# Sparse attention into a routed mixture of experts: the summary scores of a head pair in one block of four array tiles

## The chip, the core and the metric

The kernel runs on one core of a Trainium2 chip. The metric is the device time of one execution in microseconds. Before the change the median of three runs is 690.34 us (690.23 to 690.6). One execution was also recorded by the hardware profiler: it took 690.0 us, of which 688.3 us lie between the first and the last instruction (the span). The rest of this document speaks of the engines by their names in the profile: PE (the matrix engine, with PEld for its weight loads), DVE (vector), ACT (scalar), POOL and SP.

## The reference

Two things are computed one after the other.

```python
# attention: q, k, v are (4, 8, 768, 64); block = 32, window = 16
k_sum = k.reshape(B, H, nb, 32, D).max(axis=3)      # 24 block maxima of the keys
v_sum = v.reshape(B, H, nb, 32, D).mean(axis=3)     # 24 block means of the values
scores_l = scale * q @ k.T, masked to |row - col| < 16
scores_s = scale * q @ k_sum.T + log(32)            # 24 summary scores for each query
a = softmax(concat(scores_l, scores_s)); attn = a @ concat(v, v_sum)
# routing: x = attn as (3072, 512); 8 experts, hidden size 1024
P = exp(x @ w_gate - max); 8 times: divide rows by their sums, then columns, times N / E
out = sum over e of P[:, e] * (relu(x @ w1[e]) @ w2[e])
```

The change touches `scores_s` alone: for each head a product of 24 summary keys (padded to 32 rows) with 768 queries over a head size of 64.

## The kernel before

**Attention by pairs.** There are 32 heads, taken two at a time: 16 pairs `i`, four for each batch entry. The two heads of a pair are `j = 0, 1`; the transposed keys `kT`, queries `qT` and block maxima `ksT` of head `j` lie on partitions `64*j` to `64*j+63`. The 768 queries are worked on in two halves `h` of `HS` = 384. The first four pairs (`i < PB`, `pair_half`) are done half by half; the twelve others (`pair_whole`, line 634) as a whole.

For a whole pair PE does: two transposes of keys and queries into PSUM (`tr`, L282), the window scores for each half (`scores`, L301), the block sums of the values (`block_sums`, L309), the summary scores for each half (`summaries`, L387), the values for each half (`values`, L373 and L379), and a transpose of the result (`to_xT`, L473). ACT and DVE empty PSUM between these steps: ACT computes the exponentials (`score_exp` L344, `summary_exp` L397), DVE masks, makes block maxima and normalizes, and either of them does the copies (L195).

**Summary scores.** `summaries(i, h, tag)` opens one PSUM bank and issues two matmuls, one for each head. Each uses 64 rows of the array (the head's partitions) and 32 columns (the summary keys); head 0 writes PSUM partitions 0 to 31, head 1 partitions 32 to 63. So the two matmuls lie in two different tiles of the array, shape 64 x 32. The other half does the same again in another bank, in the same two tiles. `summary_exp(i, h)` then takes the exponential of partitions 0 to 63 of that bank.

**PSUM banks in the attention.** Three single banks with the tag `"a"` are handed out in turn to `tr`, `block_sums`, `summaries`, `values`, `to_xT` and `logits` of the whole pairs; one double bank `"s"` belongs to the window scores; three banks `"m"` belong to expert 0.

**Expert 0 as filler.** The first expert is computed unsplit in the same stretch of time (`expert0`, line 665): eight hidden products of four matmuls each (`hd`, L199) and three projections of eight matmuls (`pj`, L204) for each 384 tokens, as soon as the tokens' attention is done. It fills PE while attention waits for the other engines.

**What sets the order.** The class `Plan` (line 34) holds a unit for each step with its engine, an assumed cost, its dependencies, a priority and the banks that it opens or uses. It plays the units through on paper and emits them in that order; each engine then executes its own units strictly in that order. A unit that opens banks is emitted only when the previous users of those banks, in turn, are planned to be done. For copies with two possible engines the plan chooses. In the plan a call of `summaries` costs 0.22 us on PE and a `summary_exp` 0.46 us on ACT.

**The bridge.** When the last attention unit has been emitted (`logits` of the fourth batch entry, L487, and the exponential of the logits, L491), `bridge` (line 997) adds the eight row and column normalizations of `P` to the plan. Each is a chain DVE (L1007, L1008), POOL (L1011), DVE (L1015), PE (`totals`, two matmul instructions at L1020), DVE (L1023), POOL (L1028). It also adds sums of the second expert's weights and of the tokens on DVE (L765, L768: `w1_sum`, `x_sum`) and that expert's first products on PE (L818: `p1`, `p5`, `p2`, `p6`, `p3`, `p7`, `p4`). The leftover units of expert 0 stand between them. After that, from 178.6 us on, a loop with a fixed order works through experts 1 to 7 (L818, L824) by a scheme with seven instead of eight products.

Of the kernel before, what the change touches and what calls it, by code (L numbers as in the profile page):

```python
# [12 lines left out]
AF = mybir.ActivationFunctionType  # L13
# [20 lines left out]
class Plan:  # L34
# [12 lines left out]
    def add(self, eng, cost, fn, deps=(), prio=0.0, opens=(), uses=(), lag=0.0):  # L47
        u = Unit(eng, cost, fn, [d for d in deps if d is not None], prio, list(opens), lag)
        for b in list(opens) + list(uses):
            b.users.append(u)  # L50
        if uses and eng != "PE":
            u.prio -= 100.0
        self.waiting.append(u)
        return u
# [62 lines left out]
def kernel(  # L117
# [10 lines left out]
    nc = tc.nc  # L128
# [10 lines left out]
    PB = H // 2  # L139
    SCALE = 1.0 / float(D) ** 0.5  # L140
    W = 16
    LIVE = 128 + 2 * W
    PADL = LIVE + 2 * W
    HS = S // 2
# [64 lines left out]
    NB = PB  # L209
    NE = 2  # L210
# [10 lines left out]
    if True:  # L221
# [4 lines left out]
        qT = [attn.tile([128, W + S + W], BF16, name=f"qT{i}") for i in range(NB)]  # L226
        kT = [attn.tile([128, S], BF16, name=f"kT{i}") for i in range(NB)]
        ksT = [attn.tile([128, 32], BF16, name=f"ksT{i}") for i in range(NB)]
# [9 lines left out]
        add = plan.add  # L238

        at, units = {}, {}  # L240

        def bank(tag, name, dtype=FP32):
            pool, n = (mps, 3) if tag == "m" else (aps, NA)
            return pool.tile([128, 2048 // mybir.dt.size(dtype)], dtype, tag=tag, name=name, bufs=n)
# [79 lines left out]
        def near_values(i):  # L324

            sv, ve = v_x[i % NQ], V_e[i % NE]
            for j in range(2):
                c0, q0 = VD * j, 64 + 32 * j
                nc.sync.dma_start(out=ve[q0 + W:q0 + 2 * W, 1:G, c0:c0 + VD],
                                  in_=sv[128 - W:128, 0:G - 1, j, :])  # L330
                nc.sync.dma_start(out=ve[q0:q0 + W, 0:G - 1, c0:c0 + VD],
                                  in_=sv[0:W, 1:G, j, :])

        def scores(i, h):
            sg = at["sg", i, h] = banks2("sg")
            for s in range(HG):
                for j in range(2):
                    score_mm(i, sg[:, j, s * LIVE:(s + 1) * LIVE], j, HG * h + s, 0, LIVE)

        def score_exp(i, h):  # L340
            if h == 0:
                at["er", i] = attn.tile([128, 2, G, LIVE], BF16, tag="er", name="er", bufs=2)
                at["em", i] = attn.tile([128, 2, G, 128], BF16, tag="em", name="em", bufs=2)
            nc.scalar.activation(  # L344
                out=at["er", i][:, :, HG * h:HG * (h + 1), :].rearrange("p j g l -> p j (g l)"),
                in_=at.pop(("sg", i, h))[:, :, 0:HG * LIVE], func=AF.Exp, bias=0.0, scale=SCALE)

        def masks(i, h):
            c = slice(HG * h, HG * (h + 1))
            nc.vector.tensor_tensor(  # L350
                out=at["em", i][:, :, c, :], in0=at["er", i][:, :, c, W:W + 128],
                in1=band[:, None, None, W:W + 128].to_broadcast([128, 2, HG, 128]), op=ALU.mult)

        def edges(i):
            ee, er = E_e[i % NE], at.pop(("er", i))
            for j in range(2):
                q0 = 64 + 32 * j
                nc.vector.tensor_tensor(out=ee[q0:q0 + 32, 0:G - 1, 128 - W:128],
                                        in0=er[0:32, j, 1:G, 0:W],
                                        in1=band[0:32, None, 0:W].to_broadcast([32, G - 1, W]),  # L360
                                        op=ALU.mult)
                nc.vector.tensor_tensor(out=ee[q0:q0 + 32, 1:G, 0:W],
                                        in0=er[96:128, j, 0:G - 1, W + 128:LIVE],
                                        in1=band[96:128, None, W + 128:LIVE].to_broadcast([32, G - 1, W]),
                                        op=ALU.mult)

        def values(i, h):
            sv, ee, ve, em = v_x[i % NQ], E_e[i % NE], V_e[i % NE], at["em", i]
            av = at["av", i, h] = bank("a", "av")
            for cc in range(HG):  # L370
                c, o = HG * h + cc, cc * 2 * VD
                for j in range(2):
                    nc.tensor.matmul(av[:, o + j * VD:o + (j + 1) * VD],  # L373
                                     lhsT=em[:, j, c, :], rhs=sv[:, c, j, :],
                                     start=(cc == 0 and j == 0), stop=False,
                                     skip_group_check=True)
            for cc in range(HG):
                c, o = HG * h + cc, cc * 2 * VD
                nc.tensor.matmul(av[:, o:o + 2 * VD], lhsT=ee[:, c, :], rhs=ve[:, c, :],  # L379
                                 start=False, stop=True, skip_group_check=True)  # L380

        def summaries(i, h, tag):
            r = i % NB
            ss = at["ss", i, h] = bank(tag, "ss")
            for j in range(2):
                p0 = 64 * j
                nc.tensor.matmul(ss[32 * j:32 * j + 32, 0:HS], lhsT=ksT[r][p0:p0 + 64, :],  # L387
                                 rhs=qT[r][p0:p0 + 64, W + h * HS:W + (h + 1) * HS],
                                 start=True, stop=True)

        def summary_exp(i, h):
            if i < PB:
                es = at["es", i, h] = attn.tile([64, HG, 128], BF16, tag="es", name="es", bufs=2)
                dst = es[:]
            else:
                dst = E_e[i % NE][0:64, HG * h:HG * (h + 1), :]
            nc.scalar.activation(out=dst.rearrange("p g t -> p (g t)"),  # L397
                                 in_=at.pop(("ss", i, h))[0:64, 0:HS], func=AF.Exp,
                                 bias=0.0, scale=SCALE)


# [165 lines left out]
        U = {}  # L567
# [66 lines left out]
        def pair_whole(i, prio):  # L634
            U["near", i] = add("SP", 0.4, lambda: near_values(i), [U["v", i], U.get(("A", i - NE, 1))], prio,
                               lag=3.5)
            for h in range(2):
                buf = Buffer("s")
                U["S", i, h] = add("PE", 0.28, lambda h=h: scores(i, h),
                                   [U["kT", i, 0], U["kT", i, 1], U.get(("ed", i - 2))], prio, opens=[buf])  # L640
                U["X", i, h] = add("ACT", 0.97, lambda h=h: score_exp(i, h), [U["S", i, h]], prio, uses=[buf])
                U["mk", i, h] = add("DVE", 0.56, lambda h=h: masks(i, h),
                                    [U["X", i, h], U.get(("A", i - 2, 1))], prio)
            U["ed", i] = add("DVE", 0.78, lambda: edges(i),
                             [U["X", i, 0], U["X", i, 1], U["mk", i, 1], U.get(("A", i - NE, 1))], prio)
            for h in range(2):
                buf = Buffer("a")
                U["ss", i, h] = add("PE", 0.22, lambda h=h: summaries(i, h, "a"),
                                    [U["km", i], U["kT", i, 1], U.get(("A", i - NE, 1))], prio, opens=[buf])
                U["sx", i, h] = add("ACT", 0.46, lambda h=h: summary_exp(i, h), [U["ss", i, h]], prio, uses=[buf])  # L650
            for h in range(2):
                buf = Buffer("a")
                U["A", i, h] = add("PE", 0.4, lambda h=h: values(i, h),
                                   [U["mk", i, h], U["ed", i], U["sx", i, h], U["Vs", i], U["near", i]],
                                   prio, opens=[buf])
                U["no", i, h] = add("DVE", 0.68, lambda h=h: normalize(i, h),
                                    [U["A", i, h], U.get(("xt", i - 2))], prio, uses=[buf])
            buf = Buffer("a")
            U["xt", i] = add("PE", 0.35, lambda: to_xT(i), [U["no", i, 0], U["no", i, 1]], prio, opens=[buf])
            U["x", i] = add({"ACT": 0.8, "DVE": 0.9}, 0, lambda: x_out(U["x", i].on, i), [U["xt", i]], prio,  # L660
                            uses=[buf])
# [88 lines left out]
    if True:  # L750
# [340 lines left out]
        for n in range(LAG, len(groups)):  # L1091
# [3 lines left out]
            e, j, i = groups[n]  # L1095
# [61 lines left out]
        A, B, C, D = last  # L1157
# [42 lines left out]
```

## Time and profile before

| what | value |
|---|---|
| median of the runs | 690.34 us |
| profiled execution | 690.0 us, span 688.3 us |
| PE busy | 675.2 us (98%) |
| DVE busy | 588.1 us (85%) |
| ACT busy | 404.8 us (59%) |
| granted PE clock | 0.999 of full speed |
| summary score matmuls (L387) | 64, from 8.7 us to 120.9 us |
| last expert-0 matmul (L204) ends | 178.6 us |

A table by windows gives the busy time of each engine in each stretch, with the number of instructions behind it. The chain of waits lists, in order of time, the pieces of work that led to the last instruction: its start, its length, engine, tile and line. A timeline lists instructions with their start and length, and in square brackets the idle time of the engine before them and what ended it. A shape such as `64*32` is the part of the array that a matmul uses, rows by columns.

### The profile page before, as it was taken

To read this page: it belongs to the slowest core of one execution; us is meant where nothing else is said; L and a number is where in the kernel's file an instruction comes from. 1 tells how busy PE (TensorE), PEld (TensorE's weight loads), DVE (VectorE), ACT (ScalarE), POOL (GpSimd) and SP (SyncE) were. 2 spreads that over 40 slices of the span, in tenths; PEclk is the share of its full clock that TensorE was granted. 3 is DMA by queue.
4 is the path that set the end of the run, shared out by engine and by line. 5 is a ranking of instruction groups with operands and counts; after the bars stand their busy time and mean duration, and the time that the engine had idled before them with its cause. 6 is when DMAs were issued, how large, how long until landed. Compare 5 with 4: busy or idle time off the path is not lost.

```text
span 688.3 us, 13623 instructions
## 1 busy us (share of the span) xinstructions
PE 675.2 (98%) x5195; PEld 438.9 (64%) x5195; DVE 588.1 (85%) x1436; ACT 404.8 (59%) x785; POOL 140.7 (20%) x189
## 2 busy tenths in 40 slices
PE   8999999899999999999999999999999999999996
PEld 4665665445566666666666666666666666666665
DVE  6878888687599998899789988998799988998886
ACT  4677866555677775555555555555555555555551
POOL 9599920121113120110101010201010101100000
PEclk9999999999999999999999999999999999999999
DMA  9999990000233104130513050403231051301224
GB/s 131 182 131 127 128 130 6 1 1 0 31 48 32 17 7 70 17 32 1 77 12 37 1 77 1 46 2 50 28 32 16 3 75 16 32 1 47 83 88 153
DMA packets 112785, 33.90 MB, mean 49 GB/s; under 512 B 98128, under 2 KB 109904, under 8 KB 112720
## 3 DMA queue, kind: packets, MB, share of 16 engines
q0 software_dynamic: 103840, 26.22, 40.0%
q1 hardware_dynamic: 8352, 6.80, 3.3%
q8 instruction: 41, 0.67, 0.4%
q14 instruction: 24, 0.20, 0.1%
q10 hardware_dynamic: 528, 0.02, 0.0%
HBM read 52.45 MB, written 6.29 MB: 85 GB/s over the span
## 4 chain that ended last, share of the span: by engine, by line
PE 87%; DVE 11%; issue 2%; ACT 0%; DVEq 0%; ACTq 0%
PE xy L824 32%; PE pg L818 14%; PE pb L818 10%; PE pa L818 9%; PE yps L204 6%; PE hps L199 6%; DVE hf L768 3%; DVE out_acc L961 2%; PE sg L301 1%; PE tkq L282 1%; PE idle L511 1%; DVE hf L879 1%; PE ss L387 1%; PE vs L309 1%; PE tx L473 1%
## 5 line engine op out<-in xcount | busy, mean ns | idle before, releaser
L824 PEld LDWEIGHTS <-hf 128*128 128x128 f16 x2352 | 229.7, 98 | 99.2 <-issue 5.2
L824 PE MATMUL xy<-w,hf 128*128 128x256 f16 x1312 | 183.3, 272 | 0.0
L824 PE MATMUL xy<-ws,hf 128*128 128x256 f16 x984 | 147.5, 272 | 1.4
L190 ACT ACTIVATE hf<-pg 128x512 f16<-128x512 f32 x84 | 50.1, 597 | 159.6 <-PE pg L818 159.6
L961 DVE SCALAR_TENSOR_TENSOR out_acc<-xy,P_sb,out_acc 128x512 f32<-128x512 f32 x164 | 114.9, 741 | 1.7 <-PE xy L824 1.7
L765 DVE TENSOR_TENSOR hf<-hf 128x512 f16<-128x512 f16 x252 | 99.3, 421 | 3.1
L818 PE MATMUL pa<-xT,w 128*128 128x512 f16 x336 | 99.9, 379 | 0.0
L768 DVE TENSOR_TENSOR hf<-pb,c 128x512 f16<-128x512 f32 x84 | 58.0, 690 | 36.8 <-ACT xy L943 31.1
L818 PEld LDWEIGHTS <-w 128*128 128x128 f16 x672 | 65.7, 98 | 28.3 <-issue 0.5
L175 POOL DMA_DIRECT2D w<-in_moe_w_dram x56 | 42.3, 821 | 187.0 <-PE pg L818 181.5
L818 PEld LDWEIGHTS <-ws 128*128 128x128 f16 x504 | 49.3, 98 | 42.2
L190 ACT ACTIVATE hf<-pa 128x512 f16<-128x512 f32 x84 | 50.1, 597 | 21.4 <-PE pa L818 21.4
L768 DVE TENSOR_TENSOR hf<-pg,c 128x512 f16<-128x512 f32 x84 | 57.1, 679 | 0.4 <-PE pg L818 0.2
L837 ACT COPY pg<-pa 128x512 f32<-128x512 f32 x84 | 47.9, 570 | 5.1 <-PE pa L818 0.3
L818 PE MATMUL pg<-xTs,w 128*128 128x512 f16 x168 | 49.9, 379 | 0.1
L845 ACT COPY c<-pb 128x512 f32<-128x512 f32 x84 | 49.7, 592 | 0.4 <-ACT pg L837 0.4
L818 PE MATMUL pb<-xTs,ws 128*128 128x512 f16 x168 | 50.0, 379 | 0.0
L818 PE MATMUL pg<-xTs,ws 128*128 128x512 f16 x168 | 50.0, 379 | 0.0
L818 PE MATMUL pb<-xT,ws 128*128 128x512 f16 x168 | 50.0, 379 | 0.0
L818 PE MATMUL pg<-xT,w 128*128 128x512 f16 x168 | 49.8, 377 | 0.0
L852 ACT COPY c<-pg 128x512 f32<-128x512 f32 x84 | 48.7, 580 | 0.0
L199 PE MATMUL hps<-xT,w 128*128 128x384 f16 x256 | 48.6, 326 | 0.0
(133 smaller groups left out, 862.1 us busy)
## 6 DMA issues: line engine op xcount, KB each, us to landing
w<-in_moe_w_dram POOLq DMA_DIRECT2D x8, 1024.0 KB, 9.3
w<-in_moe_w_dram POOLq DMA_DIRECT2D x56, 128.0 KB, 3.5
out_dram<-out_acc SPq DMA_DIRECT2D x22, 256.0 KB, 2.0
vx<-in_v_dram POOLq DMA_DIRECT2D x32, 96.0 KB, 5.4
kst<-in_k_dram POOLq DMA_DIRECT2D x24, 96.0 KB, 4.6
qst<-in_q_dram POOLq DMA_DIRECT2D x24, 96.0 KB, 4.3
w<-in_moe_w_dram POOLq DMA_DIRECT2D x2, 512.0 KB, 8.4
kst<-in_k_dram POOLq DMA_DIRECT2D x4, 192.0 KB, 4.5
```

The lines of the kernel that those rows point to most:

```text
L175: nc.gpsimd.dma_start(out=t[:, :, h, :], in_=moe_w1[e].rearrange("(dk p) f -> p dk f", p=128)[:, :, f:f + 128])
L190: nc.scalar.activation(out=out, in_=in_, func=AF.Relu, bias=0.0, scale=1.0)
L199: nc.tensor.matmul(hp[:, 0:n], lhsT=w1s[e][:, dk, 128 * f:128 * (f + 1)], rhs=xT[:, dk, t0:t0 + n], start=(dk == 0), stop=(dk == KD - 1))
L204: nc.tensor.matmul(yp[:], lhsT=h[:, f, c * 128:(c + 1) * 128], rhs=w2s[e][:, f, :], start=(f == 0), stop=(f == KF - 1))
L765: nc.vector.tensor_tensor(out=out, in0=in0, in1=in1, op=ALU.subtract)
L768: nc.vector.tensor_tensor(out=out, in0=in0, in1=in1, op=ALU.add)
L818: nc.tensor.matmul(bank[:], lhsT=w[:, dk, :], rhs=x[:, dk, :], start=start and dk == 0, stop=dk == KH - 1, skip_group_check=True)
L824: nc.tensor.matmul(bank, lhsT=a(f)[:, 128 * c:128 * (c + 1)], rhs=w[:, f, :], start=start and f == 0, stop=f == FH - 1, skip_group_check=True)
L837: nc.scalar.copy(out=B["g"][:], in_=B["a"][:])
L845: nc.scalar.copy(out=B["c5"][:], in_=B["b"][:])
L852: nc.scalar.copy(out=B["c2"][:], in_=B["g"][:])
L961: nc.vector.scalar_tensor_tensor(out=acc, in0=src, scalar=P_sb[:, t, e:e + 1], in1=acc, op0=ALU.mult, op1=ALU.add)
```

## The change

For whole pairs the two calls of `summaries` become one call of `summaries2(i)`, which opens two banks and issues all four matmuls: half 0 writes partitions 0 to 63 of the first bank, half 1 partitions 64 to 127 of the second. The four matmuls lie in four different tiles of the array. `summary_exp` reads half 1 from partitions 64 to 127. In the plan there is one PE unit of 0.22 us in the place of two, which opens both banks; the two ACT units stay, each on its bank. The first four pairs are as before. The matmuls are the same in number and size.

```diff
+        def summaries2(i):
+            r = i % NB
+            ss = at["ss", i, 0], at["ss", i, 1] = bank("a", "ss"), bank("a", "ss")
+            for h in range(2):
+                for j in range(2):
+                    p0, o = 64 * j, 64 * h + 32 * j
+                    nc.tensor.matmul(ss[h][o:o + 32, 0:HS], lhsT=ksT[r][p0:p0 + 64, :],
+                                     rhs=qT[r][p0:p0 + 64, W + h * HS:W + (h + 1) * HS],
+                                     start=True, stop=True)
         def summary_exp(i, h):
+            o = 64 * h if i >= PB else 0
...
-                                 in_=at.pop(("ss", i, h))[0:64, 0:HS], func=AF.Exp,
+                                 in_=at.pop(("ss", i, h))[o:o + 64, 0:HS], func=AF.Exp,
...
+            bufs = [Buffer("a"), Buffer("a")]
+            U["ss", i, 0] = U["ss", i, 1] = add("PE", 0.22, lambda: summaries2(i),
+                                                [U["km", i], U["kT", i, 1], U.get(("A", i - NE, 1))], prio,
+                                                opens=bufs)
             for h in range(2):
-                buf = Buffer("a")
-                U["ss", i, h] = add("PE", 0.22, lambda h=h: summaries(i, h, "a"),
-                                    [U["km", i], U["kT", i, 1], U.get(("A", i - NE, 1))], prio, opens=[buf])
-                U["sx", i, h] = add("ACT", 0.46, lambda h=h: summary_exp(i, h), [U["ss", i, h]], prio, uses=[buf])
+                U["sx", i, h] = add("ACT", 0.46, lambda h=h: summary_exp(i, h), [U["ss", i, h]], prio,
+                                    uses=[bufs[h]])
```

## The prediction

> **What bounds the kernel now.** I first read busy time by stretches of 20 us, to see where PE, which does the changed work, has slack. Columns: stretch and its length, then PE, PEld, DVE, ACT, POOL busy, PE clock, DMA share, GB/s.
>
> ```profile
> 80.00:100.00 20.00, 20.00 (x215) 12.08 (x212) 16.16 (x45) 15.26 (x25) 10.84 (x14) 1.00 1.52 148
> 100.00:120.00 20.00, 20.00 (x235) 12.24 (x231) 16.52 (x43) 12.76 (x20) 0.00 (x0) 1.00 0.04 6
> 120.00:140.00 20.00, 16.89 (x134) 9.36 (x135) 13.63 (x42) 10.27 (x20) 2.18 (x4) 1.00 0.01 2
> 140.00:160.00 20.00, 19.98 (x107) 10.12 (x105) 16.49 (x41) 11.32 (x22) 5.25 (x10) 1.00 0.00 1
> ```
>
> All twelve changed pairs lie between 38 and 122 us, where PE is never idle while DVE and ACT have 3.5 to 7 us in 20 to spare. There PE's own time sets the pace. The one hole is 3.1 us between 120 and 140 us, the bridge. From 140 to 178.6 us PE is full again, and then comes a fixed order (509.7 us to the end) that starts when PE gets to it. So two things count: how much PE time the change removes, and what becomes of the hole.
>
> Second, what a block of summary scores costs, in the chain of waits (start, length, engine, tile, line, matmuls):
>
> ```profile
> 17.96 0.46 PE tkq L279 x12
> ...
> 48.52 0.43 PE ss L387 x4
> ...
> 53.27 0.34 PE tkq L282 x6
> 53.61 0.34 PE tx L473 x6
> 53.94 0.65 PE hps L199 x4
> 54.59 0.27 PE ss L387 x2
> 54.86 1.41 PE hps L199 x8
> 56.27 0.27 PE ss L387 x2
> 56.53 0.31 PE sg L301 x6
> ```
>
> One half alone takes 0.27 us; both halves in a row take 0.43. The tile's own view tells why:
>
> ```profile
> L387 PE MATMUL ss<-qT,ksT x64: 322/333/333, 8.7 to 120.9; 64*32 64x384 bf16 x64
> ```
>
> A matmul lasts 0.33 us from start to end, yet two pass in 0.27: the two heads stream together. The second half adds 0.16, the streaming of 384 columns; the other 0.11 is paid for leaving the tile shape (eight hidden matmuls after it take 1.41 instead of two times 0.65, again 0.11).
>
> Third, the hole, from the timeline:
>
> ```profile
> 132.58 0.36 PE L1020 MATMUL sink<-csum_sb,col_en 128*128 128x8 f32 x2 [1.42 <-DVE csum_sb L1015]
> 134.88 0.20 DVE L1023 RECIPROCAL crec_sb<-sink 128x8 f32<-128x8 f32 x1
> 138.22 0.48 DVE L1015 TENSOR_REDUCE csum_sb<-P_sb 128x8 f32<-128x192 f32 x1
> 138.76 0.39 PE L1020 MATMUL sink<-csum_sb,col_en 128*128 128x8 f32 x2 [1.69 <-DVE csum_sb L1015]
> ```
>
> PE waits twice for DVE's column sums (1.42 + 1.69 = 3.1). In the second round the reciprocal starts 2.3 us after the totals because weight and token sums stand before it in DVE's queue.
>
> **Part 1: the four tiles.** Before, six of the twelve pairs run their halves in a row (6 x 0.43) and six apart (12 x 0.27): 5.82 us. After there are twelve blocks. If all four matmuls stream together, a block is as long as one pair of them, 0.27, plus some 0.006 for two more starts: 12 x 0.276 = 3.31. Gain 2.50 us. If the halves still follow each other, it is 12 x 0.43 = 5.17, gain 0.65. Entering a shape costs too, but in the instruction order of the two kernels the changes of shape on PE fall from 143 to 137: exactly the six stretches of L387 that vanish, whose leaving is in the 0.27. So nothing more is due.
>
> Do four tiles stream together? Two tiles in different rows do (0.27). Two tiles in the same rows but different columns do as well: the early transposes L279 (128*64, head 0 in columns 0 to 63, head 1 in the others) take 0.46 for twelve, while six full ones (L282) take 0.34, so twelve in sequence would take 0.68. Two rules of the Trainium skill speak against the change. TensorEngine Tiling (Array Packing), Restrictions and Gotchas, says different row tiles cannot use the same PSUM bank at one time. Here both heads of a half share a bank, before and after; by the rule a half alone would already take 0.43, but the row says 0.27, so I drop it. TensorE: Matmul & The Clock Gate, Part 3, says a weight load overlaps a running matmul only if their row groups differ. Tiles three and four share rows with one and two; by the rule they wait and the block costs 0.43 (gain 0.65). The L279 row, same rows and a new weight load for each matmul, goes against it. I take 2.50 and keep 0.65 as the other end.
>
> ACT's exponentials (L397, 0.48 each) are as many as before and read the same number of elements. DMAs, their queues (POOL, SP) and the loads are the same in number and order; all pair loads are issued by 83 us, and pair 15's transposes come at 114 us, so an earlier PE does not catch up with them.
>
> **Part 2: the new order.** The plan sees 12 x 0.22 = 2.64 us less PE work and reorders every engine from pair 4 on. Four copies move from ACT to DVE (three of xT, one of out_acc, a net zero among the qT copies): some 0.6 us each, 2.4 us of DVE time in 85 us with 3.5 us in 20 free. I cost them at nothing; without that cover it would be up to 2.4. I looked for places where a unit now has less PE work between it and what it waits for:
>
> - Around pairs 7 to 9 expert 0 runs out: the projections of tokens 384 to 767 are used up before the next tokens exist. PE's order is here transposes of pair 9, to_xT of pair 7, transposes, block sums of 9, logits. The bank of the block sums waits for ACT's copy of the first transposes (0.80 plus about 0.25 on both sides), with only 0.34 + 0.34 of PE work between: 0.35 us lost. Bounds 0 and 1.0 (if the xT copy is late too and holds the logits).
> - The block opens two of three "a" banks, and values follow it at 1.2 us of PE work at the closest (pairs 11, 12, 15). Two exponentials need 0.9 plus 0.2, behind at most one ACT copy of 0.58; the values' first half needs only the first exponential. I put 0.2 on all twelve together; bounds 0 and 1.5.
>
> What waits behind such a stall is all of PE's queue.
>
> **Part 3: the bridge.** In the new order one more hidden product (0.65) stands before the last logits and one more between them and the first totals. The total work is the same, so I count only waits. Time from the start of the logits to the first totals was 132.55 - 129.10 = 3.45; DVE's order in it is unchanged. PE's work in it was 0.59 + 0.65 + 0.65 and is now 0.65 more: the first wait becomes 1.42 - 0.65 = 0.8. In the second round DVE's reciprocal stands behind three weight sums instead of four and two token sums and two more. From the totals: reciprocal at 0.7, POOL 0.95 to 1.6, row sums at 1.95 (after a token sum), reciprocal to 2.65, POOL to 3.35, column sums from about 4.05 (a token sum, a weight sum, a relu before it) to 4.55, totals at 4.65. PE's work between (two hidden products, p1, p5, one hidden product, p2, p6, p3 and the totals) is 0.25 + 4.1: wait 0.3. Third round by the same walk: 0.1. So the hole shrinks from 3.1 to 1.25: gain 1.85. I take 1.7, for rounding in a walk of fifteen steps. Bounds: the hole stays (0), or vanishes (3.1).
>
> **Sum.** -2.50 + 0.35 + 0.2 - 1.7 = -3.65 us. The profiled execution took 690.0 (span 688.3 and 1.7 around it), so it would be 686.35; the median lies 0.34 higher: **686.7 us**, 0.5% faster.
>
> **Rivals.**
> - *The halves still follow each other.* For it: the weight-load rule, and 0.43 with both halves in the same two tiles. Against: L279. Gain 0.65 instead of 2.50: 688.5.
> - *The hole does not shrink.* DVE's sums and POOL's turns slip in the new order, or p6 waits for its token sum: PE loses 1.85 more: 688.5.
> - *The gain is only moved.* PE reaches the main loop earlier but waits there for DVE. Against: DVE is busy 10.4 of 20 us between 160 and 180. 690.3.
> - *Slower: two of three banks at once.* Every block needs both older users emptied, and until both exponentials are done one bank serves the rest. If each of the twelve blocks costs 0.5 us, that is 6.0 - 0.2 more: 692.5. It decides from (3.65 + 0.2) / 12 = 0.32 us for each block. For it: between the transposes of pair 6 and block 5 there is only 1.3 us of PE work, and the copy takes 0.8 and its queue. Against: most blocks have 2 us or more, and the 64 matmuls of L387 had PE idle before them for 0.1 us in all.
>
> **How the numbers follow.** My forecast 0.60, halves in sequence 0.12, hole stays 0.16, gain only moved 0.06, slower 0.06. The forecast's own range is 685.7 to 687.8, from the bounds of the stalls and the hole. For 8 in 10 the two 688.5 cases have to be in: 685.4 to 689.0. About 0.2% (1.4 us) is what a measurement can tell from no change, so below 688.96 is faster. The first case and most of the next two are (0.60 + 0.10 + 0.13 = 0.83); the rest of these and the fourth are the same (0.11); 0.06 is slower.
>
> **What would show it.** Part 1: L387's successor in the new profile (its line moves to L397 and the exponential to L408) has x4 pieces of 0.27 to 0.28 in the chain; 0.43 shows it wrong. Part 2: PE idle some 0.3 to 0.6 us before block sums or logits near 69 us, nothing elsewhere up to the last logits, which start near 127.8 (129.10 - 2.5 + 0.55 + 0.65). Part 3: waits before the first three totals of about 0.8, 0.3, 0.1; the last L204 of expert 0 ends near 175. What would make it wrong: waits for ACT before the values, a DVE queue that lets p5, p6 or the totals wait longer, or a main loop that needs more than 509.7 us.

## The result

The changed kernel takes 686.59 us (median; 686.28 to 686.98), the kernel before 690.47 us in the same comparison: 3.88 us less, ratio 0.9943 with a 95% interval of 0.9926 to 0.9961. Forecast were 686.7 us. The recorded execution of the changed kernel took 686.98 us, with a span of 685.1 us.

Busy time by stretches of the changed kernel, the same four stretches and columns as shown of the kernel before:

```profile
80.00:100.00 20.00, 20.00 (x205) 12.07 (x205) 17.14 (x46) 14.07 (x23) 10.71 (x14) 1.00 1.38 126
100.00:120.00 20.00, 20.00 (x237) 12.48 (x235) 17.00 (x46) 14.96 (x25) 0.00 (x0) 1.00 0.18 29
120.00:140.00 20.00, 19.02 (x159) 10.58 (x158) 14.79 (x44) 10.22 (x21) 2.99 (x5) 1.00 0.01 2
140.00:160.00 20.00, 19.78 (x105) 10.11 (x104) 17.84 (x49) 11.29 (x22) 5.68 (x10) 1.00 0.00 1
```

PE is still full in attention, and DVE carries a little more there (17.1 against 16.2 between 80 and 100 us). The hole between 120 and 140 us has gone from 3.1 to 1.0.

The chain of waits of the changed kernel, the blocks of summary scores:

```profile
49.78 0.27 PE ss L397 x4
...
56.20 0.27 PE ss L397 x4
...
63.50 0.27 PE ss L397 x4
```

And their matmuls in the tile's own view:

```profile
L397 PE MATMUL ss<-qT,ksT x48: 332/333/333, 39.0 to 122.9; 64*32 64x384 bf16 x48
```

Four matmuls now take the 0.27 that two took; each of the four is as long as before. In the trace they start 0, 3, 7 and 10 ns after the first, and the next instruction starts 0.275 us after the first. Before it was 0.431 for four in a row.

The hole, from the timeline of the changed kernel:

```profile
131.97 0.36 PE L1033 MATMUL sink<-csum_sb,col_en 128*128 128x8 f32 x2 [0.78 <-DVE csum_sb L1028]
132.46 0.20 DVE L1036 RECIPROCAL crec_sb<-sink 128x8 f32<-128x8 f32 x1
136.20 0.48 DVE L1028 TENSOR_REDUCE csum_sb<-P_sb 128x8 f32<-128x192 f32 x1
136.74 0.39 PE L1033 MATMUL sink<-csum_sb,col_en 128*128 128x8 f32 x2 [0.20 <-DVE csum_sb L1028]
...
145.67 0.39 PE L1033 MATMUL sink<-csum_sb,col_en 128*128 128x8 f32 x2 [0.18 <-DVE csum_sb L1028]
```

The first two waits for the column sums are 0.78 and 0.20 instead of 1.42 and 1.69. They shrank for different reasons. The first column sums, one line from each kernel, first before and then after:

```profile
131.96 0.48 DVE L1015 TENSOR_REDUCE csum_sb<-P_sb 128x8 f32<-128x192 f32 x1
131.34 0.48 DVE L1028 TENSOR_REDUCE csum_sb<-P_sb 128x8 f32<-128x192 f32 x1
```

The last logits start at 129.10 before and 128.48 after, so in both kernels the column sums come 2.86 us behind them: DVE is no earlier, and the wait is 0.65 shorter because one hidden product more keeps PE busy meanwhile. In the second round it is DVE that is earlier: the reciprocal starts 0.5 us after the totals instead of 2.3, and the second totals follow the first after 4.77 us instead of 6.18, while PE's own work between them is nearly the same (4.57 and 4.49). The third totals wait no more than before, but the fourth wait 0.18, where before they waited 0.02.

To compare kernels free of the start I cut each trace at three instructions: the first block sums of pair 4, the first matmul of the last logits, and the first product of the main loop (L824, after the change L837).

| stage, us | before | after | difference |
|---|---|---|---|
| start, to block sums of pair 4 | 37.23 | 38.20 | +0.97 |
| attention, to the last logits | 91.87 | 90.28 | -1.59 |
| bridge, to the main loop | 49.29 | 46.83 | -2.46 |
| main loop to the end | 509.90 | 509.83 | -0.07 |

In the changed kernel one hidden product of 0.65 us stands ahead of the last logits that stood behind them before. Like for like, attention lost 2.24 us and the bridge 1.81. The longer start is not the change's doing: in `e7_after_bridge` (below), with the same order of attention, it took 37.25. In the execution shown the granted PE clock fell to half for 3.4 us, which may account for it; but starts of up to 38.34 were also seen with the clock at full speed.

```profile
10.00:15.00 5.00, 3.75 (x78) 2.54 (x72) 4.17 (x15) 3.04 (x5) 4.85 (x8) 0.94 1.56 170
15.00:20.00 5.00, 4.79 (x67) 2.67 (x63) 3.77 (x9) 2.69 (x4) 4.70 (x6) 0.72 1.82 177
```

These are stretches of 5 us of the changed kernel (third number from the end: PE clock); the same stretches of the kernel before have 1.00. Without the longer start the two spans would differ by 4.1 us instead of 3.15; the medians differ by 3.88.

### The profile page after: what moved, and what is told of

Same layout as the page of the kernel before. It is cut to its first block, busy times and chain, and to the rows that moved or that the text cites. A ratio compares the mean times of both kernels' runs of the same rounds, so it can differ in the third digit from the quotient of the medians.

```text
span 685.1 us, 13613 instructions
## 1 busy us (share of the span) xinstructions
PE 673.9 (98%) x5195; PEld 439.0 (64%) x5195; DVE 590.4 (86%) x1440; ACT 404.7 (59%) x781; POOL 141.5 (21%) x189
## 4 chain that ended last, share of the span: by engine, by line
PE 85%; DVE 10%; issue 2%; DMA 1%; POOL 1%; ACT 0%; DVEq 0%; ACTq 0%
PE xy L837 32%; PE pg L831 14%; PE pb L831 9%; PE pa L831 9%; PE yps L204 6%; PE hps L199 6%; DVE hf L781 3%; DVE out_acc L974 2%; PE sg L301 1%; PE tkq L282 1%; DVE hf L892 1%; PE vs L309 1%; DVE hf L778 1%; DMA vx<-in_v_dram 1%; PE av L446 1%
## 5 line engine op out<-in xcount | busy, mean ns | idle before, releaser
L837 PEld LDWEIGHTS <-hf 128*128 128x128 f16 x2352 | 229.8, 98 | 99.2 <-issue 5.2
L837 PE MATMUL xy<-w,hf 128*128 128x256 f16 x1312 | 183.4, 273 | 0.0
L837 PE MATMUL xy<-ws,hf 128*128 128x256 f16 x984 | 147.6, 272 | 1.4
```

The lines of the kernel that those rows point to most:

```text
L837: nc.tensor.matmul(bank, lhsT=a(f)[:, 128 * c:128 * (c + 1)], rhs=w[:, f, :], start=start and f == 0, stop=f == FH - 1, skip_group_check=True)
```

## The experiments

Three accounts were to be told apart: the time comes from the tiles; it comes from the new order, above all from the smaller hole; or the hole shrinks merely because attention got shorter. Times are medians. Measured beside the first four runs, the kernel before took 690.43 us; beside the last four, 690.85 us. As the start differs by up to 3 us from execution to execution, the stages of the profiled executions decide where the medians are close.

| kernel | median | ratio to before, 95% | attention | bridge | waits before the first two totals |
|---|---|---|---|---|---|
| before | 690.43 | | 91.87 | 49.29 | 1.42, 1.69 |
| changed | 686.59 | 0.9943 [0.9926, 0.9961] | 90.28 * | 46.83 | 0.78, 0.20 |
| e1_same_tiles | 688.61 | 0.9969 [0.9956, 0.9982] | 92.15 * | 46.83 | 0.78, 0.20 |
| e2_offset | 689.82 | 0.9995 [0.9984, 1.0005] | 90.94 | 49.30 | 1.43, 1.69 |
| e3_cost28 | 688.39 | 0.9980 [0.9968, 0.9991] | 89.43 | 49.30 | 1.42, 1.69 |
| e4_before_bridge | 689.08 | 0.9976 [0.9969, 0.9982] | 91.87 | 47.55 | 1.22, 0.67 |
| e5_after_late_sums | 688.20 | 0.9960 [0.9947, 0.9972] | 90.28 * | 48.50 | 1.85, 1.40 |
| e6_one_bank | 686.85 | 0.9941 [0.9924, 0.9958] | 91.01 ** | 46.11 | 0.77, under 0.15 |
| e7_after_bridge | 685.47 | 0.9926 [0.9905, 0.9948] | 90.28 * | 45.12 | 0.58, under 0.15 |
| e8_one_bank_bridge | 684.78 | 0.9909 [0.9896, 0.9923] | 91.01 ** | 44.73 | 0.57, under 0.15 |

(* with one, ** with two hidden products of 0.65 us moved from the bridge into attention.)

**The same order, without the four tiles.**

```diff
-                    p0, o = 64 * j, 64 * h + 32 * j
+                    p0, o = 64 * j, 32 * j
...
-            o = 64 * h if i >= PB else 0
+            o = 0
```

> The changed kernel with both query halves in the same two array tiles (partitions 0 to 63 of each half's own bank); the order of all engines is that of the changed kernel. It splits the gain into tiles and order. Theory (2.50 us of the gain are the tiles): each of the twelve blocks takes 0.43 in place of 0.275 us, 12 x 0.156 = 1.9 us slower than the changed kernel: 688.5 us, and 1.9 faster than before by the new order alone (hole in the bridge still about 1.2 us). Rival (the time comes from the order, the tiles are hidden): 686.6, as the changed kernel. Rival (the tiles are nearly all): 690.

Measured: 688.61 us. From the chain of waits of this kernel:

```profile
51.98 0.43 PE ss L397 x4
52.41 0.31 PE sg L301 x6
...
58.55 0.43 PE ss L397 x4
58.98 0.32 PE sg L301 x6
```

With the halves in the same two tiles a block is back at 0.43 (the third matmul starts 173 ns after the first). Attention takes 92.15 instead of 90.28, 1.87 us more, which is 12 x 0.156; bridge and waits are those of the changed kernel to the hundredth. So the tiles, in this order, are worth 1.9 us, and the new order with its single unit, without the tiles, already 1.8 (2.2 by the two stages: 1.81 in the bridge and 0.37 in attention).

**The tiles, without the new order.**

```diff
-                p0 = 64 * j
-                nc.tensor.matmul(ss[32 * j:32 * j + 32, 0:HS], lhsT=ksT[r][p0:p0 + 64, :],
+                p0, o = 64 * j, 32 * j + (64 * h if i >= PB else 0)
+                nc.tensor.matmul(ss[o:o + 32, 0:HS], lhsT=ksT[r][p0:p0 + 64, :],
...
-                                 in_=at.pop(("ss", i, h))[0:64, 0:HS], func=AF.Exp,
+                                 in_=at.pop(("ss", i, h))[o:o + 64, 0:HS], func=AF.Exp,
```

> The kernel before, its two units per pair and its whole order kept; only the second half writes partitions 64 to 127 of its bank, that is, lies in the other two tiles. Theory: the six pairs whose halves stand in a row go from 0.43 to 0.275, 6 x 0.156 = 0.94 us; the six others stay at 2 x 0.27; the hole in the bridge stays at 3.1: 689.4 to 689.5 us. Rival (tiles need one unit to stream together, or the gain vanishes in the hole): 690.4. Rival (the tiles bring all of the changed kernel's gain): below 688.

Measured: 689.82 us, which its interval does not separate from no change. The chain of waits of this kernel shows what happened:

```profile
49.08 0.27 PE ss L387 x4
...
55.00 0.27 PE ss L387 x2
55.26 1.41 PE hps L199 x8
56.67 0.27 PE ss L387 x2
```

Halves in a row now take 0.27 together, halves apart still 0.27 each. Attention falls by 0.93 us (0.94 expected), and the bridge is unchanged. Two units that happen to stand next to each other stream together as well; what the single unit adds is that it makes all twelve stand so.

**The tiles with another order.**

```diff
-            U["ss", i, 0] = U["ss", i, 1] = add("PE", 0.22, lambda: summaries2(i),
+            U["ss", i, 0] = U["ss", i, 1] = add("PE", 0.28, lambda: summaries2(i),
```

> The changed kernel with the plan's cost of the new block set to 0.28 us, about what it takes, in place of 0.22. The matmuls are the same; the planned order becomes another, and in the bridge it falls back on that of the kernel before (four weight sums and two token sums ahead of the reciprocal). Theory (a good half of the gain is the smaller hole, which the new order brings by chance): the hole is back at about 3 us, 1.9 more than in the changed kernel: 688.5 us. Rival (the hole shrank because PE's attention got shorter, whatever the order): 686.6.

Measured: 688.39 us. The hole, from this kernel's timeline:

```profile
130.59 0.36 PE L1033 MATMUL sink<-csum_sb,col_en 128*128 128x8 f32 x2 [1.42 <-DVE csum_sb L1028]
132.88 0.20 DVE L1036 RECIPROCAL crec_sb<-sink 128x8 f32<-128x8 f32 x1
136.77 0.39 PE L1033 MATMUL sink<-csum_sb,col_en 128*128 128x8 f32 x2 [1.69 <-DVE csum_sb L1028]
```

Attention is the shortest of all, like for like: 2.44 us less than before with the same work in it, so the gain of the blocks arrives in full and no new wait eats into it (PE is idle nowhere in it). But the bridge has the order of the kernel before again, and with it the same two waits to the hundredth. A plan that is told nearly the true cost of the block is 1.8 us slower (1.6 by the two stages) than one that is told too little. So the smaller hole does not follow from a shorter attention; it goes with the order.

**The hole alone, in the kernel before.**

```diff
-                for eng, us, fn, o, w in (("DVE", 0.5, rows, (), ()), ("POOL", 0.7, by_rows, (), ()),
-                                          ("DVE", 0.35, columns, (), ()), ("PE", 0.12, totals, [buf], ()),
-                                          ("DVE", 0.2, inverse, (), [buf]), ("POOL", 0.7, by_columns, (), ())):
+                for eng, us, fn, o, w in (("DVE", 0.7, rows, (), ()), ("POOL", 0.65, by_rows, (), ()),
+                                          ("DVE", 0.45, columns, (), ()), ("PE", 0.2, totals, [buf], ()),
+                                          ("DVE", 0.25, inverse, (), [buf]), ("POOL", 0.65, by_columns, (), ())):
...
-                    X[j, n] = add("DVE", 0.65, lambda j=j, n=n: x_sum(j, n),
+                    X[j, n] = add("DVE", 0.7, lambda j=j, n=n: x_sum(j, n),
...
-                    Wt[i, n] = add("DVE", 0.26, lambda i=i, n=n: w1_sum(1, i, n), [Wt.get((i, n - 1))],
+                    Wt[i, n] = add("DVE", 0.32, lambda i=i, n=n: w1_sum(1, i, n), [Wt.get((i, n - 1))],
```

> The kernel before with the summary scores untouched; only the plan's assumed costs in the bridge are changed (token sum 0.70, weight sum 0.32, row sums 0.70, POOL 0.65, column sums 0.45, totals 0.20, reciprocal 0.25), so that the attention's order stays word for word and the column sums and the reciprocal stand behind fewer weight and token sums. Theory (the hole is made by what stands ahead of them in DVE's queue): first wait 1.4 to 1.1, second 1.7 to about 0.5 to 1.0, in all 0.9 to 1.5 us faster: 689.2 us. Rival (the hole comes from the length of the normalization chain itself): 690.4.

Measured: 689.08 us. Attention is that of the kernel before (91.87), the bridge 1.74 us shorter. From the timeline:

```profile
132.54 0.36 PE L1020 MATMUL sink<-csum_sb,col_en 128*128 128x8 f32 x2 [1.22 <-DVE csum_sb L1015]
134.23 0.20 DVE L1023 RECIPROCAL crec_sb<-sink 128x8 f32<-128x8 f32 x1
137.69 0.39 PE L1020 MATMUL sink<-csum_sb,col_en 128*128 128x8 f32 x2 [0.67 <-DVE csum_sb L1015]
```

Fewer sums ahead of DVE's column sums and reciprocal are enough to shrink the hole, with no change to the summary scores. The two waits account for 1.2 of the 1.74 us; the rest are delays at later totals, too short to be listed as waits, which come up again below.

**The hole alone, in the changed kernel, the other way.**

```diff
-                    Wt[i, n] = add("DVE", 0.26, lambda i=i, n=n: w1_sum(1, i, n), [Wt.get((i, n - 1))],
+                    Wt[i, n] = add("DVE", 0.1, lambda i=i, n=n: w1_sum(1, i, n), [Wt.get((i, n - 1))],
```

> The changed kernel with one assumed cost in the plan altered: a weight sum counts 0.10 us in place of 0.26, so the plan packs more of them ahead of the column sums and the reciprocal (first column sums behind eight weight sums and a token sum in place of four weight sums). Attention and its order stay. Theory (the hole is what stands ahead in DVE's queue): first column sums some 2 us later, of which one hidden product more ahead of the totals covers 0.65; first wait 0.8 to about 2.1, later waits as before or a little longer: 1.3 to 2.5 us slower than the changed kernel, 688 to 689 us. Rival (the hole shrank since attention is shorter): 686.6.

Measured: 688.20 us, attention unchanged at 90.28, the bridge 1.67 us longer. From the timeline:

```profile
133.45 0.36 PE L1033 MATMUL sink<-csum_sb,col_en 128*128 128x8 f32 x2 [1.85 <-DVE csum_sb L1028]
...
138.69 0.39 PE L1033 MATMUL sink<-csum_sb,col_en 128*128 128x8 f32 x2 [1.40 <-DVE csum_sb L1028]
```

The first column sums come 1.7 us later behind the logits than in the changed kernel (4.58 against 2.86), and the first wait grows as expected, with one hidden product more to cover it. The total came out as expected too; the second wait did not: it was expected nearly unchanged and grew by 1.2. The second totals follow the first after 5.24 us instead of 4.77, and the hidden product that now stands ahead of the first totals is missing between the two. So more sums ahead of DVE's links of the chain make a larger hole, and where PE's filler stands decides how much of it shows.

**One bank for the four tiles.**

```diff
-            ss = at["ss", i, 0], at["ss", i, 1] = bank("a", "ss"), bank("a", "ss")
+            t = bank("a", "ss")
+            ss = at["ss", i, 0], at["ss", i, 1] = t, t
...
-            bufs = [Buffer("a"), Buffer("a")]
+            bufs = [Buffer("a")]
...
-                                    uses=[bufs[h]])
+                                    uses=bufs)
```

> The changed kernel with the four tiles of a pair in one PSUM bank: half 0 on partitions 0 to 63, half 1 on 64 to 127 of the same bank; the plan opens one bank instead of two and the order becomes another. It asks whether a bank for each half is needed. Theory (tiles stream together whatever the bank): each block 0.275 us; the bridge keeps a reciprocal behind three weight sums, so the hole stays near 1.2: 686 to 687 us. Rival (four tiles in one bank follow each other): 0.43 a block, 1.9 us more: 688.5. Rival (two of three banks at once cost waits in the changed kernel): below 686.

Measured: 686.85 us. All twelve blocks have their four starts within 10 ns; what follows starts 0.275 us after the first in all but one. There the keys' transposes of the next pair start 0.28 us late, and the queries' transposes behind them wait 0.34 us for the exponentials (PE is idle in attention for 0.67 us in all, against 0.20 in the changed kernel). So a bank for each half is not what lets the tiles stream together. Counted with the same hidden products in it, attention takes 89.71 here and 89.63 in the changed kernel; as the order is another one, with seven changes of tile shape fewer, this does not show what two banks cost. The changed kernel's own trace does: PE is never idle there at a block or at the values behind it.

**Less of the hole in the changed kernel.** The edit of `e4_before_bridge`, made in the changed kernel.

> The changed kernel with the bridge's assumed costs set as in the run on the kernel before (token sum 0.70, weight sum 0.32, row sums 0.70, POOL 0.65, column sums 0.45, totals 0.20, reciprocal 0.25). Attention's order stays. Theory: column sums behind three weight sums in place of four (first wait 0.8 to 0.5) and the second wait 0.2 to 0: 0.4 to 0.6 us faster than the changed kernel, 686.1 us. Rival (what is left of the hole is the chain's own length): 686.6. Rival (token sums come later and p5 or p6 waits for them): 687 or more.

Measured: 685.47 us. Bridge 45.12, 1.71 us less than in the changed kernel, where 0.4 to 0.6 was expected. The direction held; the size did not, because I had counted only the two large waits. In the trace of the changed kernel, time between PE starts beyond what the matmuls themselves need adds up to 2.1 us in the bridge: 0.9 and 0.4 at the first two totals, 0.35 and 0.2 at two later ones, and small ones. Here it is 0.7, all at the first totals, whose wait now ends with ACT by the profile. (In these traces late totals cost 0.16 more than the idle time listed before them: 0.94 for a listed 0.78, 0.74 for a listed 0.58.) The executions of this kernel scatter from 683.97 to 689.07, so its median alone says little.

**Both together.** The edits of `e6_one_bank` and `e7_after_bridge`.

> One bank for the four tiles and the bridge's assumed costs together. Theory (both are independent): 685.8 to 686.5 us, the first wait about 0.5. Rival (another order, another hole): as the changed kernel or slower.

Measured: 684.78 us (684.55 to 684.96), 0.9% less than before and the lowest median of all. It beat the expectation by about 1 us; here too the bridge shrank more than the two waits that had been counted. That it lies below e7 is not one bank's doing: attention and bridge together take 135.74 us here and 135.40 in e7 (137.11 in the changed kernel, 137.12 in e6), and the difference in the medians is within e7's scatter.

## Why the prediction was right

**The bound.** PE's time sets the pace in attention: e1 adds 1.87 us of PE time there and gets 1.87 us of length. The main loop took 509.83 after 509.90.

**Part 1, the tiles.** Forecast 2.50 us; e3, the same work in an order with no new wait, shows 2.44. The block takes 0.275 (forecast 0.276) and the halves apart are gone. Both rules that spoke against do not hold here: two row tiles of one bank start 3 to 4 ns apart and take 0.27 together, four tiles in one bank take 0.275 (e6), and tiles that share rows start 7 ns apart although each has its own weight load. The count of shape changes (six fewer, already in the 0.27) held: nothing more was gained.

**Part 2, the new order.** Forecast 0.55 us of new waits. The one at the block sums of pair 9 was there, for the copy of the first transposes as foretold, with 0.20 instead of 0.35. This is its line in the timeline of the changed kernel:

```profile
70.06 0.51 PE L309 MATMUL vs<-vx,m_blk 128*64 128x128 bf16 x6 [0.20 <-ACT kT L195]
```

The 0.2 for the blocks with two banks did not show; PE never waited at them. The whole term, 0.55 against 0.20, was 0.35 too large. DVE's cover was thinner than stated: between 60 and 80 us it was busy 17.35 of 20 us before the change, which leaves 2.65 and not 3.5. Putting the moved copies at nothing held all the same: e3 shows no idle PE in attention, and the changed kernel only the 0.20.

**Part 3, the bridge.** Forecast 1.7 (1.85 by the walk), measured 1.81: first wait 0.8 (0.78), second 0.3 (0.20), third 0.1 (none). The fourth wait of 0.18 was not in the walk, so its total of about 1.2 (1.16 measured) is in part luck. The cause was right in both halves: a hidden product more ahead of the first totals, and fewer sums ahead of the reciprocal in the second round. e4 and e5 move DVE's sums and show that half from both sides, though the plan also moved PE's units there; e3 takes both halves away together. No run tests the hidden product alone; its share is read from the timelines.

**The sum.** Terms as measured: -2.44, +0.20 for waits, -1.81 for the bridge, -0.07 for the loop, in all -4.1, against -3.65. The medians fell by 3.88. The difference between -4.1 and -3.88 is within what the start scatters. So the stages gained about 0.5 us more than forecast, mostly from the 0.35 too much in part 2, and that the median came within 0.1 us of 686.7 is in part luck.

**The rivals.** Halves in sequence: the block is 0.275, and e1 shows what it would have cost (688.61, forecast 688.5). The hole stays: e3 made it (688.39, forecast 688.5). The gain only moved: the main loop did not grow. Slower by two banks: PE was not idle at any block.

Right by its own steps, then; but nearly half of the gain is a matter of order that another assumed cost (0.28 instead of 0.22) takes away.

## What to carry to other kernels

Small matmuls in four different tiles of the array (64 x 32 with 384 columns here) cost what two do, 0.275 against 0.27 us, provided they stand next to each other in PE's queue; where an order is planned, make them one unit. When a change alters a planned order, read the new order of every engine and add up what becomes of each wait: here the bridge was worth nearly as much as the edit itself, and it could be had without the edit. Before settling on the costs that a plan assumes, try some: by the two stages, a truer one was slower by 1.6 us, and truer ones in another place faster by 1.7.

## What the runs showed of the hardware

Four tiles in one PSUM bank, written at the same time by four matmuls, took as long (0.275 us) as four tiles in two banks.

The length of the start differs from execution to execution, whatever the kernel: the block sums of pair 4 started between 37.2 and 40.2 us in the ten profiled executions. In two of them the granted clock fell to half early: for 3.4 us from 14.4 us on in the changed kernel (block sums at 38.20) and for 6.8 us from 16.1 us on in e1 (40.24, the latest of all). In e6 they came at 38.34 with no such fall, so the clock is not all of the scatter. Stretches of 5 us of e1:

```profile
15.00:20.00 5.00, 4.94 (x60) 2.98 (x62) 3.82 (x9) 2.55 (x4) 3.68 (x5) 0.61 1.86 176
20.00:25.00 5.00, 5.00 (x67) 3.08 (x61) 3.10 (x9) 3.13 (x5) 3.47 (x5) 0.70 1.25 209
```

PE is busy only 3.68 to 4.13 of the 5 us between 10 and 15 us in all ten. Whether this idle time lets the clock fall was not tested; it does not decide alone, since the kernel before, with 3.68 like e1, kept its clock.
